# Reordering a cast, moving one stage by a slot, and halving the last tile in a linear attention and mixer kernel

## The chip, the core and the metric

One core of a Trainium2 chip. Times are device microseconds of one execution; lower is better. All runs told here are fast (granted TensorE clock 0.995 to 1.0). Below, PE is TensorE, PEld its weight loads, DVE is VectorE, ACT is ScalarE, POOL is GpSimd, SP is SyncE; a "q" after the name is that engine's instruction queue where it issues a DMA.

## The reference

Eight batches, eight heads, 576 rows, 64 columns per head. Linear attention, then a token mixer and a channel mixer:

```python
k_p, q_p = phi(k), phi(q)                    # phi(x) = elu(x) + 1
kv  = einsum('bhsd,bhse->bhde', k_p, v);  z = k_p.sum(axis=2)
x   = einsum('bhsd,bhde->bhse', q_p, kv) / (einsum('bhsd,bhd->bhs', q_p, z)[..., None] + 1e-6)
# heads side by side: x is [8, 576, 512]
h   = relu(x.T @ w_tok1) @ w_tok2;  u = x + h.T          # token mixer
out = u + relu(u @ w_ch1) @ w_ch2                        # channel mixer, 512 -> 1536 -> 512
```

## The kernel before

The program is a hand-made order: a list of large pieces of PE work ("big": blocks of the channel mixer), and between them, at numbered slots, the small pieces of the next batch ("fill"). Each slot of the channel mixer is four matmuls of 512 columns. Batches go in pairs, as the last 64 rows of two batches share one tile.

Names used below: k' and q' are `k_p` and `q_p`; kv is the product of k' and v; the numerators (nd) are the products of q' with kv and z; mm1 and mm2 are the two products of the token mixer; uT is u transposed, uTt the same for the tile of the tail rows that two batches share; cr and crt are relu(u @ w_ch1), again for whole tiles and for the tail. PSUM is the memory that PE writes its results to; to evict a block is to copy it from there, which frees its buffer. A "row" of a timeline is a run of like instructions merged into one line.

```python
def vcast(n, c, copy=nc.scalar.copy):            # L151: v to bf16, beside a column of ones
    copy(out=vs[:, js, :, 0:D], in_=raw["v", n % 2][:, js]...)

def kv(n, cs):                                   # L169: 72 quarter matmuls, c = 0 then c = 1
    for c in cs:
        for t in range(T):
            for a, i in QUARTERS:
                nc.tensor.matmul(out=ps[half[i], a, c], lhsT=kp[half[a], c, t, i],
                                 rhs=vs[half[a], 2 * c + i, t], ...)
    ...                                          # L175: two ACT copies into kvbd

def mm3(n, mc, kjs=range(NDM), dve=False):       # one block of the channel mixer, L475
    if kjs[0] == 0:
        part_of[mc] = ps_big.tile([128, 512], FP32, name="c_ps", tag="big")    # 4 buffers
    ...
    if kjs[-1] == NDM - 1 and dve:
        nc.vector.tensor_scalar(out=cr[b][:, mc, :], in0=ps, ..., op0=ALU.max)  # L479
    elif kjs[-1] == NDM - 1:
        nc.scalar.activation(out=cr[b][:, mc, :], in_=ps, func=AF.Relu)         # L482

# batch 1 prepared beside batch 0 (slots at0): qt0 11, qt1 13, vc 13, kv 14, ...
late = [("vc", lambda: vcast(1, 0)), ("vc", lambda: vcast(1, 1, nc.vector.tensor_copy))]
for nm, fn in first[1:3] + late + first[0:1] + first[3:]:     # first = kv, qt0, qt1, nd...
    fill += [(at0[nm], fn)]

# batch 2 prepared beside batch 1; DVE evicts blocks 4 and 7 (counted from 0)
big = ... + [lambda mc=mc: mm3(1, mc, dve=mc in (4, 7)) for mc in range(3, NCH)] + m3t + m4(0, [4, 5, 6, 7, 8])
at1 = {"kv": 7, "nd00": 9, ..., "mm1": 16, "mm2a": 17, "mm2b": 18, "mm2t": 20, "uta": 17, "utb": 18}
fill = [(s, lambda g=g: phi("k", 2, g)) for g, s in ((0, 0), (1, 2))]
fill += [(4, lambda: vcast(2, 0)), (5, lambda: vcast(2, 1, nc.vector.tensor_copy))]
# [...]
# last pair: tiles of the second channel product in the order 8, 4, 5, 6, 7; each one ends in
nc.vector.tensor_tensor(out=o, in0=ps, in1=u[b][:, r, :], op=ALU.add)           # L518
# and one store of 64 rows on SP and one on ACT                                  # L523
```

## Time and profile before

| | before |
|---|---|
| time, median of the runs of the first measurement | 267.39 us (266.95 to 267.62, 4 runs) |
| span in the profile | 265.8 us |
| PE busy | 256.6 us, 97% |
| PE waits on the cast of v | 0.8 us, two times |

How to read it: PE is full, so the span is PE's work plus its gaps plus the two ends (the start before PE's first useful matmul, and the add and the store after its last).

### The profile page before, as it was taken

Reading aid. Unit: us, or ns where it says so; the run is one execution under the profiler, and the core shown is the slowest. Engines: PE = TensorE matmul, PEld = TensorE weight load, DVE = VectorE, ACT = ScalarE, POOL = GpSimd, SP = SyncE. Lnnn points to the kernel's source line nnn. Section 1 sums busy time; section 2 is a strip of 40 time slices with the busy share of each in tenths; the row PEclk is TensorE's granted clock in tenths of the full one; section 3 lists DMA queues with packets and bytes.
Section 4 is the critical chain, followed back from the end, with each engine's and each line's share of the span. In section 5 each row is a group of like instructions: output and inputs, shape, how many; then the busy total and the mean of one; then the engine's idle time right before and its main releaser. Section 6 shows DMA issues by size and latency. Waiting matters only on the chain.

```text
span 265.8 us, 5142 instructions
## 1 busy us (share of the span) xinstructions
PE 256.6 (97%) x2107; PEld 134.1 (50%) x2107; DVE 158.2 (60%) x311; ACT 132.8 (50%) x200; POOL 33.4 (13%) x54
## 2 busy tenths in 40 slices
PE   7999989999999999999999999999999999999992
PEld 2684445554744454455554554455564554444641
DVE  5764967966839686948684286939684272320121
ACT  5645768268464358525771358435870363036300
POOL 9720300120002300030001300030001300000000
PEclk9999999999999999999999999999999999999999
DMA  7999999399406995899999990671074500730043
GB/s 260 246 203 280 373 214 399 133 191 402 168 2 125 191 383 201 108 239 369 285 411 210 258 409 32 143 171 36 2 135 116 118 2 0 162 94 2 0 118 79
DMA packets 49927, 48.34 MB, mean 182 GB/s; under 512 B 30256, under 2 KB 35248, under 8 KB 49904
## 3 DMA queue, kind: packets, MB, share of 16 engines
q1 hardware_dynamic: 41824, 35.53, 46.8%
q0 software_dynamic: 7440, 11.44, 20.4%
q10 hardware_dynamic: 640, 1.05, 1.2%
q8 instruction: 16, 0.26, 0.4%
q14 instruction: 7, 0.06, 0.1%
HBM read 35.85 MB, written 9.44 MB: 170 GB/s over the span
## 4 chain that ended last, share of the span: by engine, by line
PE 87%; DMA 4%; DVE 3%; ACT 2%; issue 1%; POOL 0%; ACTq 0%; POOLq 0%
PE h_ps L501 34%; PE c_ps L475 27%; PE a_ps L248 5%; PE h_ps L261 5%; DMA uTt<-ut 4%; PE c_ps L489 4%; PE bank L545 3%; PE nd_ps L210 3%; PE kv_ps L169 2%; ACT e L125 1%; PE bank L363 1%; PE bank L413 1%; DVE e L139 1%; DVE vs L151 1%; PE bank L385 1%
## 5 line engine op out<-in xcount | busy, mean ns | idle before, releaser
L482 ACT ACTIVATE cr<-c_ps 128x512 bf16<-128x512 f32 x91 | 53.5, 598 | 78.0 <-PE c_ps L475 77.8
L475 PE MATMUL c_ps<-uT,wc 128*128 128x512 bf16 x384 | 91.5, 379 | 0.4 <-ACT uT L444 0.4
L501 PE MATMUL h_ps<-wc,cr 128*128 128x512 bf16 x384 | 87.4, 379 | 0.0
L501 PEld LDWEIGHTS <-cr 128*128 128x128 bf16 x384 | 37.1, 98 | 43.0
L475 PEld LDWEIGHTS <-wc 128*128 128x128 bf16 x384 | 35.7, 98 | 36.5 <-issue 1.0
L518 DVE TENSOR_TENSOR o_sb<-h_ps,u 128x512 f32<-128x512 f32 x32 | 21.8, 688 | 28.0 <-PE h_ps L501 27.9
L523 POOL DMA_DIRECT2D out_dram<-o_sb x24 | 14.9, 627 | 154.1 <-DVE o_sb L518 154.1
L222 DVE TENSOR_TENSOR x<-nd_ps,den 128x512 bf16<-128x512 f32 (+1 forms) x42 | 25.3, 602 | 1.4
L139 DVE TENSOR_SCALAR e<-e 128x1152 bf16<-128x1152 bf16 x30 | 13.9, 463 | 12.7 <-ACT e L125 12.6
L125 ACT ACTIVATE e<-k_raw 128x1152 bf16<-128x1152 f32 x16 | 18.7, 1170 | 2.3 <-DMA k_raw<-in_k_dram 2.3
L125 ACT ACTIVATE e<-q_raw 128x1152 bf16<-128x1152 f32 x16 | 18.5, 1161 | 1.6 <-DMA q_raw<-in_q_dram 1.4
L273 DVE TENSOR_TENSOR u<-h_ps,x 128x1024 bf16<-128x1024 f32 x12 | 14.4, 1219 | 7.2 <-PE h_ps L261 7.1
L219 DVE TENSOR_SCALAR den<-nd_ps 128x8 f32<-128x8 f32 (+1 forms) x42 | 6.8, 163 | 19.2 <-PE nd_ps L210 18.6
L261 PE MATMUL h_ps<-ar,w2p 128*128 128x512 bf16 x60 | 16.0, 379 | 0.1
L210 PEld LDWEIGHTS <-qT 128*128 128x128 bf16 x140 | 11.4, 98 | 9.3 <-issue 0.2
L210 PE MATMUL nd_ps<-kvbd,qT 128*128 128x130 bf16 x140 | 15.1, 223 | 0.0
L248 PE MATMUL a_ps<-x,w 128*128 128x512 bf16 x56 | 14.4, 379 | 0.0
L151 ACT CAST vs<-v_raw 128x1152 bf16<-128x1152 f32 x12 | 13.9, 1160 | 0.0
L528 DVE TENSOR_TENSOR o_sb<-h_ps,ut 128x512 f32<-128x512 f32 x4 | 2.8, 690 | 18.7 <-PE h_ps L501 18.7
L251 ACT ACTIVATE ar<-a_ps 128x512 bf16<-128x512 f32 x14 | 7.6, 595 | 12.1 <-PE a_ps L248 12.1
L140 DVE TENSOR_TENSOR qp<-e,y 128x1152 bf16<-128x1152 bf16 x16 | 12.1, 758 | 0.6
L131 DVE TENSOR_SCALAR y<-q_raw 128x1152 bf16<-128x1152 f32 x16 | 12.1, 756 | 0.3
(102 smaller groups left out, 218.1 us busy)
## 6 DMA issues: line engine op xcount, KB each, us to landing
k_raw<-in_k_dram SPq DMA_DIRECT2D x16, 576.0 KB, 9.0
q_raw<-in_q_dram SPq DMA_DIRECT2D x16, 576.0 KB, 7.0
v_raw<-in_v_dram SPq DMA_DIRECT2D x14, 576.0 KB, 11.0
out_dram<-o_sb POOLq DMA_DIRECT2D x24, 256.0 KB, 4.7
wc<-in_moe_w_ch_dram POOLq DMA_DIRECT2D x8, 384.0 KB, 9.8
out_dram<-o_sb SPq DMA_DIRECT2D x10, 128.0 KB, 2.3
out_dram<-o_sb ACTq DMA_DIRECT2D x8, 128.0 KB, 2.6
out_dram<-o_sb POOLq DMA_DIRECT2D x6, 128.0 KB, 7.0
```

What stands on the lines that cost most here:

```text
L125: nc.scalar.activation(out=e, in_=f, func=AF.Exp)
L139: nc.vector.tensor_scalar(out=e, in0=e, scalar1=1.0, scalar2=None, op0=ALU.min)
L151: copy(out=vs[:, js, :, 0:D], in_=raw["v", n % 2][:, js].rearrange("p j (t d) -> p j t d", t=T))
L210: nc.tensor.matmul(out=o[:, a], lhsT=qT[b][:, t0:t0 + 128], rhs=kvbd[b][:, c, a], start=True, stop=True)
L222: nc.vector.tensor_tensor(out=x[b][:, rs[0]:rs[0] + m, HG * D * g:HG * D * (g + 1)].rearrange("p r (h d) -> p r h d", h=HG), in0=v_[:, :, ...
L248: nc.tensor.matmul(out=ps[:, mt], lhsT=w1t[:, b, ms] if r == R else w1[:, r, ms], rhs=x[b][:, r, :], start=(r == 0), stop=(r == R))
L261: nc.tensor.matmul(out=ps[:, i], lhsT=w2v(kt, r, b), rhs=ar[b][:, kt, :], start=(kt == 0), stop=(kt == NT - 1 and not add))
L475: nc.tensor.matmul(out=ps, lhsT=wc1[:, kj, 128 * mc:128 * mc + 128], rhs=uT[b][:, :, kj], start=(kj == 0), stop=(kj == NDM - 1))
L482: nc.scalar.activation(out=cr[b][:, mc, :], in_=ps, func=AF.Relu)
L501: nc.tensor.matmul(out=ps, lhsT=crt[:, kc, :] if t == 8 else cr[b][:, kc, 128 * r:128 * r + 128], rhs=wc2[:, kc, :], start=(kc == 0), stop ...
L518: nc.vector.tensor_tensor(out=o, in0=ps, in1=u[b][:, r, :], op=ALU.add)
L523: (nc.scalar if last and e else put).dma_start(out=outv[2 * p + b, :, 2 * r0 + e:2 * r0 + e + 2 * m - 1:2], in_=live["o"][half[e], 0:m])
```

## The change

Three parts: the cast of v in batch 1 goes ahead of the copies of q' (so that DVE casts while PE transposes); kv of batch 2 goes one slot later with everything that hangs on it; and the very last tile is computed, added and stored in two halves of 256 columns.

```diff
+    def mm4_last(c):
+        p, b, r, cs = B // 2 - 1, 1, R - 1, COLS[c]
+        ps = ps_big.tile([128, 512], FP32, name="h2_ps", tag="big")[:, 0:DM // 2]
+        for kc in range(NCH):
+            nc.tensor.matmul(out=ps, lhsT=cr[b][:, kc, 128 * r:128 * r + 128],
+                             rhs=wc2[:, kc, cs], start=(kc == 0), stop=(kc == NCH - 1))
+        o = outp.tile([128, 2, DM], FP32, name="o_sb", tag="o_sb")[:, 0, 0:DM // 2]
+        nc.vector.tensor_tensor(out=o, in0=ps, in1=u[b][:, r, cs], op=ALU.add)
+        for e in range(2):
+            (nc.scalar if e else nc.sync).dma_start(out=outv[2 * p + b, :, 2 * r + e, cs],
+                                                    in_=o[half[e]])
-    for nm, fn in first[1:3] + late + first[0:1] + first[3:]:
+    for nm, fn in first[1:2] + late + first[2:3] + first[0:1] + first[3:]:
-    at1 = {"kv": 7, "nd00": 9, "nd01": 10, "nd10": 11, "nd11": 12, "nd20": 13, "nd21": 14,
-           "mm1": 16, "mm2a": 17, "mm2b": 18, "mm2t": 20, "uta": 17, "utb": 18}
+    at1 = {"kv": 8, "nd00": 10, "nd01": 11, "nd10": 12, "nd11": 13, "nd20": 14, "nd21": 15,
+           "mm1": 17, "mm2a": 18, "mm2b": 19, "mm2t": 21, "uta": 18, "utb": 19}
-    fill += [(s, lambda g=g: phi("q", 3, g)) for g, s in ((0, 19), (1, 21))]
-    fill += [(22, lambda: qtr_dma(3)), (22, lambda: load_all(4, "qkv"))]
-    fill += [(s, lambda g=g: prep_k(3, g)) for g, s in ((0, 24), (1, 26))]
+    fill += [(s, lambda g=g: phi("q", 3, g)) for g, s in ((0, 19), (1, 22))]
+    fill += [(23, lambda: qtr_dma(3)), (23, lambda: load_all(4, "qkv"))]
+    fill += [(s, lambda g=g: prep_k(3, g)) for g, s in ((0, 24), (1, 27))]
-            big = m3(n) + m3t + m4(p, [4, 5, 6, 7, 8] if n + 1 < B else [8, 4, 5, 6, 7])
+            big = m3(n) + m3t + m4(p, [4, 5, 6, 7, 8])
+            if n + 1 == B:
+                big = m3(n) + m3t + m4(p, [8, 4, 5, 6]) + [lambda: mm4_last(0), lambda: mm4_last(1)]
```

The lines of the changed kernel after this function are numbered 13 higher; the two new lines that count are 537 (matmul) and 540 (add), with the stores at 542.

## The prediction

> **What bounds the kernel now.** I read the page first (busy shares, chain of waits), then the waits of TensorE after the start-up, then the timeline around each place that the change touches. The change is a matter of tenths of a microsecond, so shares do not decide it; single instructions do.
>
> The page, span and busy shares:
>
> ```profile
> span 265.8 us, 5142 instructions
> PE 256.6 (97%) x2107; PEld 134.1 (50%) x2107; DVE 158.2 (60%) x311; ACT 132.8 (50%) x200; POOL 33.4 (13%) x54
> ```
>
> TensorE (PE) is busy 97% of the span, and the chain of waits is PE for 87% of it. So PE's work is the floor, and only two things can be gained: gaps between PE's instructions, and what comes before its first and after its last matmul. The waits of PE alone, from 20 us to the end (who waited for whom: us in total, times, longest), the three largest:
>
> ```profile
> PE kv_ps L169 <- DVE vs L151: 0.8, 2, 0.5
> PE tp L180 <- DVE qp L140: 0.6, 2, 0.4
> PE c_ps L475 <- ACT uT L444: 0.4, 1, 0.4
> ```
>
> The largest is the product k'v (line 169) waiting for VectorE's cast of v (line 151), two times: in batch 1 and in batch 2. The first two parts of the change aim at these. Timeline of batch 1 (start us, duration us, engine, line, output<-input, count, idle before):
>
> ```profile
> 36.21 0.76 DVE L140 TENSOR_TENSOR qp<-e,y 128x1152 bf16<-128x1152 bf16 x1
> 37.54 1.03 PE L501 MATMUL h_ps<-wc,cr 128*128 128x512 bf16 x4
> 37.74 0.82 DVE L187 COPY qT<-tp 128x640 bf16<-128x640 bf16 x2 [0.77 <-PE tp L180]
> 38.48 0.75 DVE L151 CAST vs<-v_raw 128x1152 bf16<-128x1152 f32 x1
> 38.50 0.48 PE L169 MATMUL kv_ps<-vs,kp 64*64 64x65 bf16 x36
> 39.29 0.48 PE L169 MATMUL kv_ps<-vs,kp 64*64 64x65 bf16 x36 [0.30 <-DVE vs L151]
> 39.70 1.04 PE L501 MATMUL h_ps<-wc,cr 128*128 128x512 bf16 x4
> ```
>
> VectorE (DVE) idles 0.77 us for PE's transposes, copies them out, and only then casts v; the second 36 matmuls start right as the cast ends. Batch 2:
>
> ```profile
> 62.32 0.68 DVE L479 TENSOR_SCALAR cr<-c_ps 128x512 bf16<-128x512 f32 x1
> 62.70 0.48 PE L169 MATMUL kv_ps<-vs,kp 64*64 64x65 bf16 x36
> 62.92 0.75 DVE L151 CAST vs<-v_raw 128x1152 bf16<-128x1152 f32 x1
> 63.73 0.48 PE L169 MATMUL kv_ps<-vs,kp 64*64 64x65 bf16 x36 [0.54 <-DVE vs L151]
> 64.14 1.41 PEld L475 LDWEIGHTS <-wc 128*128 128x128 bf16 x8
> 64.14 1.90 PE L475 MATMUL c_ps<-uT,wc 128*128 128x512 bf16 x8
> ```
>
> Here DVE is busy all the way: the eviction of the fifth channel block (line 479) and then the cast. A kv without a wait, batch 3:
>
> ```profile
> 79.26 1.23 DVE L273 TENSOR_TENSOR u<-h_ps,x 128x1024 bf16<-128x1024 f32 x1 [0.50 <-PE h_ps L261]
> 88.99 1.89 PE L475 MATMUL c_ps<-uT,wc 128*128 128x512 bf16 x8
> 89.56 0.76 DVE L140 TENSOR_TENSOR kp<-e,y 128x1152 bf16<-128x1152 bf16 x1
> 90.81 0.78 PE L169 MATMUL kv_ps<-vs,kp 64*64 64x65 bf16 x72
> 91.52 1.90 PE L475 MATMUL c_ps<-uT,wc 128*128 128x512 bf16 x8
> ```
>
> All 72 run together, and from kv's start to the next matmul it is 91.52 - 90.81 = 0.71 us. But k' of batch 3 is ready (89.56 + 0.76 = 90.32) only 0.49 us before kv begins. Finally the end:
>
> ```profile
> 261.15 0.69 DVE L518 TENSOR_TENSOR o_sb<-h_ps,u 128x512 f32<-128x512 f32 x1 [1.90 <-PE h_ps L501]
> out_dram<-o_sb SPq DMA_DIRECT2D x3, 128.0 KB, 2.3
> out_dram<-o_sb ACTq DMA_DIRECT2D x3, 128.0 KB, 2.6
> ```
>
> After PE's last matmul one add of 0.69 us and a store that lands after 2.3 and 2.6 us lie bare.
>
> **What the Trainium skill says.** "TensorE: Matmul & The Clock Gate", section "Step-by-step: what each phase is for": matmuls stay in program order, only weight loads are pulled ahead. So a kv that waits holds everything behind it, as above. The same page, "Back-to-back issue gap", gives N/2.4 + 2.5 ns: 216 ns for 512 columns, 109 ns for 256. The trace agrees: eight 512-column matmuls take 1.73 us in the chain (0.216 each), twenty 256-column ones at line 413 take 2.18 us (0.109 each). "VectorE: DVE Perf Modes", the section on the TRN2 errata, gives (N + 151)/0.96 ns for an fp32 tensor_tensor add: 691 ns for 512, 424 ns for 256. The trace has 688 and 690 ns at lines 518 and 528, and 424 ns for the 128x256 form of line 222, also a read of PSUM. "DMA: Bandwidth & Descriptors", "Latency and other measured facts", puts a fixed cost of about 2 us on a DMA, most of it the receipt from HBM; so halving a store saves only the moving part. Here that part is visible: in half-microsecond windows after 262.0 the DMA share is 0, 0.08, 0.90, 0.96, 0.07, so about 1.0 us of moving.
>
> **The change part by part.** The order of instructions on each engine, built for both kernels, shows little more than the diff: on DVE the cast of batch 1 moves ahead of its two qT copies and nothing else moves except the last add; ScalarE (ACT) has one eviction more before kv's copies in batch 2; PE has the batch 2 chain one slot of four 512-column matmuls later.
>
> *A, batch 1.* q' ends at 36.97. The cast can start then: v was issued at 19.7 and 20.3 us and landed at most 14.6 us later, by about 34.9. It runs to about 37.7, while DVE was idle for the transposes anyway, so the qT copies still start at about 37.74. kv's first half keeps 38.50 (PE's four matmuls of 37.54 stream until 38.41). The second half follows at once: next matmul at 38.50 + 0.71 = 39.21 in place of 39.70. Gain 0.49 us. What follows (kvbd copies on ACT, numerators, q' of batch 2) hangs on PE and moves with it; q of batch 2 lands at an absolute time (ACT starts its exponential at 43.23 after a wait for the DMA), but DVE needs that result only at 47.74, with more than 2 us of slack.
>
> *B, batch 2.* The last four matmuls ahead of kv start at 61.66 and stream to 61.66 + 4 x 0.216 = 62.52. A kv without waits would end at 62.52 + 0.09 + 0.71 = 63.32, where the next matmul now starts at 64.14: the two waits cost 0.82 us. But with kv a slot later, the ninth channel block comes first, and it takes the PSUM buffer of the fifth (four buffers in rotation; the built order shows that it waits on DVE). DVE frees that at 62.32 + 0.68 = 63.00. So PE starts at about 63.06 and not 62.52, streams to 63.92, and runs kv with v cast (63.67) by then: to 63.92 + 0.09 + 0.71 = 64.72. Before, the same point (kv and ninth block done) was 64.14 + 0.86 = 65.00. Gain 0.28 us in place of 0.82.
>
> *C, what B hands on to batch 3.* Numerators, first mixer product and its u now come after one more slot: 0.86 later in program order, less the 0.28: 0.58 us later in time. From the u at 79.26 to k' at 90.32 DVE has no gap in the timeline: seventeen instructions, whose durations sum to 11.9 us in a stretch of 11.06 (each starts a little before the modelled end of the one before). So k' ends at 90.90 relative to A's shift, with the semaphore (0.06 us from the cast's end to kv in batch 2) 90.96. PE gets to kv of batch 3 at 90.81 - 0.28 = 90.53, and its second half 0.29 us later, 90.82. It waits about 0.14 us. B and C together: 0.28 - 0.14 = 0.14 us. Later batches resynchronise (DVE idles 2.77 us for PE before the numerators of batch 3).
>
> *D, the end.* 24 matmuls of 256 columns take 24 x 0.109 = 2.62 us in place of 12 x 0.216 = 2.59: lost 0.02. The last add: 0.69 to 0.42, gained 0.27. The last store: half the bytes in as many pieces (64 rows on each of two queues, 1 KB in place of 2 KB). If the moving time halves, 0.5 us; if it goes by pieces, nothing; I take 0.3, an estimate. The first half's store is issued about 1.3 us earlier and out of the way. Sum 0.55 us.
>
> Total: 0.49 + 0.14 + 0.55 = 1.18 us. 267.51 - 1.18 = 266.3 us.
>
> **The rivals.** (1) No new wait: B gains the full 0.82 and C nothing. Then 267.51 - 0.49 - 0.82 - 0.55 = 265.65. For it speaks that steady batches show kv without any wait; against it, DVE's eviction at 62.32, which nothing in the change moves. (2) DVE becomes the bound: the shift of B falls on the gapless stretch from 79 to 90 us and costs as much at kv of batch 3 as B gained. Then 266.5. It is the closest rival; 0.14 us here is the difference of numbers near 90 with errors of about 0.1 each. (3) The store is all fixed latency, and its end does not move: D gains 0.25 and the time is 266.6. (4) A is hidden by a landing of q or by DVE's own load between 41 and 51 us: 266.8. Against it: DVE's numerator rhythm there is PE's (1.10 us for four matmuls and four short ones), and no transfer is waited for by PE.
>
> **Range and chances.** All rivals lie between 265.65 and 266.8; runs of the kernel before spread over 0.34 us. I put 8 in 10 on 265.7 to 266.9. Two per cent is 5.35 us, more than four times the largest sum, and nothing on the path can cost as much: faster 0.01, same 0.98, slower 0.01.
>
> **What would show it.** A right: kv of batch 1 as 72 matmuls in one row, no wait for the cast. B right: the wait of kv for the cast gone, and in its place about half a microsecond of PE before the ninth channel block, put down to DVE line 479. C right: a short stop inside kv of batch 3, put down to k'. D right: a last add of 0.42 us, and the last store landing in about 2.0 to 2.4 us. I am wrong if DVE starts the chain of batch 2 at another time relative to PE (B and C change together), or if a transposing DMA that now starts 0.58 us later holds up the numerators of batch 3.

## More of the kernel before

One more stretch of the chain of waits (start us, us, what) was there to be read, and comes back later:

```profile
119.69 11.95 DMA uTt<-ut
131.68 1.05 PE c_ps L489 x16
```

It is the transposing DMA for the tail rows of batches 2 and 3. PE was busy nearly all the time that it was in flight, so it looked harmless.

## The result, and the profile after

| | before | after |
|---|---|---|
| median, first measurement | 267.39 us (4 runs) | 266.34 us (265.98 to 266.39, 4 runs) |
| ratio of fast runs, 95% interval | | 0.9960 (0.9942 to 0.9977) |
| measured once more, in the last set of runs | 267.63 us (11 runs) | 266.09 us (265.83 to 266.47, 6 runs) |
| ratio, 95% interval | | 0.9944 (0.9931 to 0.9958) |
| span in the first profile | 265.8 us | 264.5 us |

A ratio is the mean time of one kernel's fast runs over that of the other's of the same rounds, so not quite the ratio of the medians. The time for before, 267.51, was the median of three runs; the fourth made it 267.39.

The waits of PE in the changed kernel from 20 us on (who waited for whom: us in total, times, longest), the second and third of six:

```profile
PE c_ps L475 <- ACT uT L444: 0.4, 1, 0.4
PE c_ps L475 <- DVE cr L479: 0.4, 1, 0.4
```

Both waits for the cast (line 151) are gone. The second of these lines is new: it is the wait on the eviction at line 479. (The list counts 0.38 us from the modelled end of the matmul before; the ninth block could have followed that matmul 0.216 us after its start, at 62.36, so PE lost 0.54 us.) The timeline of batch 1 in the changed kernel (start us, duration us, engine, line, output<-input, count, idle before):

```profile
37.21 0.76 DVE L151 CAST vs<-v_raw 128x1152 bf16<-128x1152 f32 x1
...
38.82 0.78 PE L169 MATMUL kv_ps<-vs,kp 64*64 64x65 bf16 x72
39.53 1.04 PE L501 MATMUL h_ps<-wc,cr 128*128 128x512 bf16 x4
```

The cast now runs at 37.21, while PE transposes (37.35 to 38.03); the copies follow at 38.06. So all 72 matmuls of kv stand in one row: 39.53 - 38.82 = 0.71 us to the next matmul, where it was 1.20. Batch 2:

```profile
62.16 0.68 DVE L479 TENSOR_SCALAR cr<-c_ps 128x512 bf16<-128x512 f32 x1
...
62.90 1.02 PE L475 MATMUL c_ps<-uT,wc 128*128 128x512 bf16 x4 [0.38 <-DVE cr L479]
...
63.85 0.78 PE L169 MATMUL kv_ps<-vs,kp 64*64 64x65 bf16 x72
```

PE waits for the eviction to end (62.84) and starts at 62.90; the cast (62.76 to 63.51) is then in time for kv at 63.85. The next block starts at 64.56. Batch 3:

```profile
89.98 0.76 DVE L140 TENSOR_TENSOR kp<-e,y 128x1152 bf16<-128x1152 bf16 x1
90.36 0.91 PE L169 MATMUL kv_ps<-vs,kp 64*64 64x65 bf16 x72
```

kv of batch 3 takes 0.91 where a kv without a stop takes 0.78. No wait is listed for it, and the 72 stay merged into one row, as the stop is too short for both views; only the duration, and k' ending at 90.74 after kv's start, show it. The end of the kernel, first the timeline and then the issues of stores (KB each, median us from issue to landing):

```profile
260.69 0.42 DVE L540 TENSOR_TENSOR o_sb<-h_ps,u 128x256 f32<-128x256 f32 x1 [0.89 <-PE h_ps L537]
```

```profile
out_dram<-o_sb SPq DMA_DIRECT2D x2, 64.0 KB, 2.0
out_dram<-o_sb ACTq DMA_DIRECT2D x2, 64.0 KB, 2.3
```

The add fell from 0.69 to 0.42. The landing times just above are medians over both halves' stores. For the last half alone they are 1.9 (SP) and 2.2 us (ACT), where the last whole tile of the kernel before took 2.3 and 2.6: 0.4 less.

**Where the time is, stretch by stretch.** Whole times differ by 1 us and more between runs of one kernel (before alone: 266.98 to 267.96 in one set; eviction first: 264.69 to 266.25), so tenths can't be read from them. Stretches of PE's timeline can. I cut every profile at the same matmuls: the first matmul of kv in batch 1; the first of the token mixer of batch 1 (line 248); the first of kv of batch 4; of kv of batch 5; the first of the tail tile of the last pair (line 501, from crt); the end of the last add; the end of the span.

| run | start to kv 1 | kv 1 to mixer 1 | to kv 4 | kv 4 to kv 5 | to the last tiles | to the last add's end | to the end |
|---|---|---|---|---|---|---|---|
| before | 38.50 | 8.49 | 69.98 | 32.59 | 98.44 | 13.84 | 3.96 |
| after | 38.82 | 8.01 | 69.83 | 32.40 | 98.45 | 13.60 | 3.39 |
| after, again | 38.52 | 8.00 | 69.85 | 32.30 | 98.45 | 13.61 | 3.38 |
| cast alone | 39.11 | 8.01 | 69.98 | 32.30 | 98.45 | 13.85 | 3.91 |
| slot alone | 37.95 | 8.49 | 69.84 | 32.55 | 98.44 | 13.85 | 3.99 |
| tail alone | 39.18 | 8.49 | 69.99 | 32.64 | 98.45 | 13.60 | 3.36 |
| mixer back | 39.24 | 8.01 | 69.70 | 32.45 | 98.45 | 13.61 | 3.45 |
| eviction first | 39.07 | 8.01 | 69.15 | 32.78 | 98.44 | 13.61 | 3.44 |
| DVE more, in after | 38.99 | 8.01 | 70.64 | 32.30 | 98.44 | 13.60 | 3.42 |
| DVE more, in before | 38.34 | 8.49 | 70.05 | 32.65 | 98.44 | 13.84 | 3.89 |
| all, cut at 384 | 38.61 | 8.01 | 69.01 | 32.30 | 98.45 | 13.47 | 3.55 |
| loads later | 39.11 | 8.01 | 69.83 | 32.31 | 98.45 | 13.60 | 3.40 |
| best | 38.70 | 8.00 | 69.02 | 32.30 | 98.45 | 13.60 | 3.44 |

(The spans are given to a tenth, so the last column is good to 0.1.) In seven of these traces (after again, cast, slot, tail, mixer back, loads later, best) the first of the twelve matmuls of the tail tile has no record: the trace shows eleven, after a gap of 0.27 us where the others show 0.06. There the cut is set 0.216 us before the first one recorded. Four columns repeat to 0.02 us wherever the kernels agree in them. Two vary from trace to trace for other reasons: the start, where the differences arise ahead of the instructions that the edits touch, and the stretch between kv of batch 4 and of batch 5, of which more below.

### The profile page after: what moved, and what is told of

It is laid out like the page before. It is cut to its first block, busy times and chain, and to the rows that moved or that the text cites. A ratio compares the mean times of both kernels' runs of the same rounds, so it can differ in the third digit from the quotient of the medians.

```text
span 264.5 us, 5173 instructions
## 1 busy us (share of the span) xinstructions
PE 255.8 (97%) x2119; PEld 135.0 (51%) x2119; DVE 158.3 (60%) x312; ACT 132.8 (50%) x200; POOL 33.0 (12%) x54
## 4 chain that ended last, share of the span: by engine, by line
PE 87%; DVE 5%; DMA 3%; ACT 2%; POOL 1%; issue 1%; ACTq 0%; POOLq 0%
PE h_ps L501 34%; PE c_ps L475 27%; PE a_ps L248 6%; PE h_ps L261 5%; PE c_ps L489 4%; PE nd_ps L210 3%; DMA cr<-in_v_dram 3%; PE kv_ps L169 2%; DVE y L131 1%; PE h_ps L537 1%; DVE cr L479 1%; DVE kp L140 1%; PE bank L363 1%; PE bank L413 1%; DVE e L139 1%
## 5 line engine op out<-in xcount | busy, mean ns | idle before, releaser
L501 PE MATMUL h_ps<-wc,cr 128*128 128x512 bf16 x372 | 84.9, 379 | 0.0
L501 PEld LDWEIGHTS <-cr 128*128 128x128 bf16 x372 | 36.0, 98 | 41.3
L518 DVE TENSOR_TENSOR o_sb<-h_ps,u 128x512 f32<-128x512 f32 x31 | 21.1, 688 | 23.1 <-PE h_ps L501 23.0
L139 DVE TENSOR_SCALAR e<-e 128x1152 bf16<-128x1152 bf16 x30 | 13.9, 462 | 12.5 <-ACT e L125 12.4
```

The source lines that it names most:

```text
L139: nc.vector.tensor_scalar(out=e, in0=e, scalar1=1.0, scalar2=None, op0=ALU.min)
L501: nc.tensor.matmul(out=ps, lhsT=crt[:, kc, :] if t == 8 else cr[b][:, kc, 128 * r:128 * r + 128], rhs=wc2[:, kc, :], start=(kc == 0), stop ...
```

## The experiments

**Each part alone.** Three kernels: before with the changed order of the cast only; before with the changed at1, phi, transposing and k' slots only; before with mm4_last only. Their edits are the corresponding hunks of the diff above. First the cast:

```diff
-    for nm, fn in first[1:3] + late + first[0:1] + first[3:]:
+    for nm, fn in first[1:2] + late + first[2:3] + first[0:1] + first[3:]:
```

> Part A alone (cast of v ahead of q's copies in batch 1). Theory: kv of batch 1 runs as one row of 72, the next matmul starts 0.71 us after kv's first in place of 1.20, so 0.49 us less than the kernel before (267.4 to 266.9), with nothing else moved. Rival (the copies of q' or the landing of q give it back before the numerators): under 0.15 us less.

Measured: kv of batch 1 is one row of 72, and the stretch to the mixer is 8.01 in place of 8.49 us: 0.48 us gained, all of it kept up to kv of batch 4 (69.98, as before). The time, 267.23 against 267.42 us, ratio 0.9995 (0.9982 to 1.0008), doesn't resolve it: the interval goes from a gain of 0.48, just what the trace shows, to a loss of 0.21 us. In its profile the start took 0.6 us more than in before's, ahead of anything that the cast can touch.

Then the slot (the hunks of at1, phi q, qtr_dma, load_all and prep_k):

```diff
-    at1 = {"kv": 7, "nd00": 9, [...] "mm1": 16, "mm2a": 17, "mm2b": 18, [...]}
+    at1 = {"kv": 8, "nd00": 10, [...] "mm1": 17, "mm2a": 18, "mm2b": 19, [...]}
```

> Part B alone (kv of batch 2 one slot later with its whole chain). Theory: the cast's wait (0.54) goes, a wait of about 0.4 for the eviction on VectorE line 479 comes, and kv of batch 3 stops 0.1 to 0.2 us for k': net 0.14 us less than before (0.0 to 0.3). Rival (no new waits): 0.82 us less. Rival (the chain into batch 3 takes all): 0 or more time.

Measured: 69.84 in place of 69.98, so 0.14 us, with both new waits in the timeline: 0.38 us for line 479 before the ninth block, and a kv of batch 3 of 0.91 us. The time shows no gain: 267.59 against 267.42, ratio 1.0011 (0.9996 to 1.0025). That speaks against 0.82 us, and is a hair outside of 0.14 (the interval ends at a gain of 0.11). I hold to the trace for the stretch and leave open whether chance at the start made these six runs slow.

Then the tail (mm4_last and the last list of big):

```diff
+            if n + 1 == B:
+                big = m3(n) + m3t + m4(p, [8, 4, 5, 6]) + [lambda: mm4_last(0), lambda: mm4_last(1)]
```

> The halved last tile alone. Theory: the last add is 0.42 in place of 0.69 us, the last store lands 0.3 us sooner after its issue, PE loses 0.03: 0.54 us less than before. Rival (the store is fixed latency): 0.25 us less.

Measured: from the last tiles to the end of the last add 13.60 in place of 13.84, and from there to the end 3.36 in place of 3.96 us. The time is 266.87 against 267.42, ratio 0.9979 (0.9963 to 0.9995), 0.56 us gained with 0.13 to 0.99 in the interval. This is the only part whose gain the times show by themselves.

The times of the three parts together give 0.13 - 0.29 + 0.56 = 0.40 us, where their stretches give 1.4 and the whole change measured 1.07 and 1.5. Chance at the start is large enough for that difference, but with one trace of each kernel it is not shown to be the reason. What follows on single parts rests on the stretches.

**Where the second store's gain comes from.** The DMA engines' share of time at the end (columns after the window: its length, then busy us of PE, PEld, DVE, ACT, POOL with counts, granted clock, DMA share, GB/s), before:

```profile
263.00:263.60 0.60, 0.00 (x0) 0.00 (x0) 0.00 (x0) 0.00 (x0) 0.00 (x0) 1.00 0.95 188
263.60:264.20 0.60, 0.00 (x0) 0.00 (x0) 0.00 (x0) 0.00 (x0) 0.00 (x0) 1.00 0.66 236
```

and after:

```profile
261.80:262.40 0.60, 0.00 (x0) 0.00 (x0) 0.00 (x0) 0.00 (x0) 0.00 (x0) 1.00 0.20 44
262.40:263.00 0.60, 0.00 (x0) 0.00 (x0) 0.00 (x0) 0.00 (x0) 0.00 (x0) 1.00 0.78 174
```

Share times length, over these windows and one before them in before's trace with a share of 0.06: 1.0 us of moving before, 0.6 after. Both traces have 128 pieces for the last store, of 2048 bytes (123 ns each on average) and of 1024 bytes (72 ns). So the moving falls with the bytes, though not quite to half, and not with the number of pieces. From the first piece to the last it takes 262.98 to 264.16 us before and 262.26 to 263.00 after, 0.44 less, and the ACT store lands 0.42 sooner after its issue (2.64 to 2.22). The rest of this stretch's gain, some 0.1 us, comes after the landing: from there to the end of the span it is 1.27 to 1.30 us in the four traces with a whole last tile and 1.15 to 1.18 in all with a cut one. No run here shows why.

**Is the stop in kv of batch 3 that chain?** First the mixer of batch 2 put back to its old slots, kv and numerators left one slot later:

```diff
-           "mm1": 17, "mm2a": 18, "mm2b": 19, "mm2t": 21, "uta": 18, "utb": 19}
+           "mm1": 16, "mm2a": 17, "mm2b": 18, "mm2t": 20, "uta": 17, "utb": 18}
-    fill += [(s, lambda g=g: phi("q", 3, g)) for g, s in ((0, 19), (1, 22))]   # [...] 23, 27
+    fill += [(s, lambda g=g: phi("q", 3, g)) for g, s in ((0, 19), (1, 21))]   # [...] 22, 26
```

(Cut: qtr_dma and load_all go back from slot 23 to 22 and the second prep_k from 27 to 26.)

> The changed kernel with the token mixer's products of batch 2, its transposes and the preparation of batch 3 put back to the slots that they had before; kv and the numerators stay one slot later. Theory: u of batch 2 is 0.86 us earlier against PE's other work, so k' of batch 3 is ready before kv and its stop goes: 0.14 us less than the changed kernel, 1.2 to 1.3 less than before. The wait for line 479 stays. Rival (the stop in kv of batch 3 has nothing to do with that chain, or mm1 now waits for the last numerators): no gain, or a new wait of PE at line 248.

Measured: 69.70 in place of 69.83 us, and kv of batch 3 lasts 0.78 again (start 90.78, with k' ending at 90.30):

```profile
90.78 0.78 PE L169 MATMUL kv_ps<-vs,kp 64*64 64x65 bf16 x72
```

The wait for line 479 stays at 0.4. 0.13 us gained, no new wait at line 248. The time is 0.9958 (0.9942 to 0.9973) of before.

Then the suspected cost doubled: one DVE instruction of the gapless stretch is repeated (it writes a y that nobody reads, so the result stays right), in the changed kernel and in the one before.

```diff
-    fill += [(s, lambda g=g: prep_k(3, g)) for g, s in ((0, 24), (1, 27))]
+    fill += [(24, lambda: prep_k(3, 0)), (24, lambda: phi_add("k", 3, 0, 2)), (27, lambda: prep_k(3, 1))]
```

> The changed kernel with one VectorE instruction of 0.75 us repeated (idempotent, its result unused) inside the gapless stretch ahead of k' of batch 3. Theory: the stop in kv of batch 3 grows by the start-to-start time of such an instruction, 0.67 us, to about 0.8 us, and the kernel with it. Rival (the stretch isn't what kv waits for): no change.

Measured: kv of batch 3 falls in two.

```profile
90.54 0.48 PE L169 MATMUL kv_ps<-vs,kp 64*64 64x65 bf16 x36
90.95 0.76 DVE L140 TENSOR_TENSOR kp<-e,y 128x1152 bf16<-128x1152 bf16 x1
91.76 0.48 PE L169 MATMUL kv_ps<-vs,kp 64*64 64x65 bf16 x36 [0.74 <-DVE kp L140]
```

The second half starts 1.22 us after the first, where 0.29 is enough: a stop of 0.93 us. The stretch is 70.64 in place of 69.83, so 0.81 us more, somewhat over the 0.67 expected: from the repeat's start to the next one's it is 0.67, but the instruction ahead of it, at 87.60, also holds DVE longer, 0.80 us to the repeat at 88.40, where it was 0.68 without. The time loses half or more of what the change had gained (0.998 of before, 0.9967 to 0.9993).

> The kernel before with the same repeated instruction at the same place. Theory: there kv's second half had 0.29 + 0.43 = 0.72 us of slack, so 0.67 us more on VectorE costs 0.0 to 0.1 us. Rival: it costs what it costs in the changed kernel.

Measured: in the kernel before, the same instruction costs 70.05 - 69.98 = 0.07 us; kv of batch 3 lasts 0.85 in place of 0.78. Time 0.9995 (0.9983 to 1.0007) of before. The repeat puts DVE back by 0.79 us here (the instruction ahead of it holds DVE for 0.79 us, 86.86 to 87.65, in place of 0.68, and the repeat itself for 0.68), and the slack was 0.72: the 0.49 us between k' and kv that the prediction read, plus 0.29 to kv's second half, less 0.06 for the semaphore. The difference is the 0.07. So the slack was there, and the changed kernel had used it up.

**Is the wait at line 479 a matter of order?** The changed kernel, but the second half of k' is made after the fifth block's eviction, not before it:

```diff
-    fill = [(s, lambda g=g: phi("k", 2, g)) for g, s in ((0, 0), (1, 2))]
+    fill = [(0, lambda: phi("k", 2, 0)), (2, lambda: phi_exp("k", 2, 2, 2)),
+            (4, lambda: phi_add("k", 2, 2, 2)), (4, lambda: phi_end("k", 2, 2, 2))]
```

> The changed kernel, but VectorE evicts the fifth channel block of batch 2 (line 479) before it makes the second half of k', not after. Theory: the PSUM buffer comes free about 1.3 us sooner, so the ninth block needn't wait (0.4 to 0.5 us of PE gained), and the cast ends when it did, just in time for kv's second half: 0.4 to 0.55 us less than the changed kernel. Rival (the wait only moves to the cast or to k'): under 0.1 us gained, with a wait inside kv of batch 2.

Measured: 69.15 in place of 69.83 us, 0.68 gained, more than expected. The timeline of batch 2:

```profile
56.85 6.64 PE L475 MATMUL c_ps<-uT,wc 128*128 128x512 bf16 x30
...
60.39 0.68 DVE L479 TENSOR_SCALAR cr<-c_ps 128x512 bf16<-128x512 f32 x1
...
62.82 0.76 DVE L151 CAST vs<-v_raw 128x1152 bf16<-128x1152 f32 x1
...
63.42 0.78 PE L169 MATMUL kv_ps<-vs,kp 64*64 64x65 bf16 x72
```

The eviction comes 60.39 - 56.85 = 3.54 us after the start of that row of matmuls, where it was 62.16 - 56.60 = 5.56 in the changed kernel; the thirty matmuls ahead of kv run without a break (29 x 0.216 + 0.38 = 6.64), and kv's second half starts about when the cast ends. The 0.68 is 0.54 for the wait at line 479 and 0.14 for a shorter one that the prediction had not counted: the eighth block too had waited for its buffer (26 matmuls took 5.92 us in before and after, where 25 x 0.216 + 0.38 is 5.78). In the built order of this kernel the eighth block takes the buffer that DVE frees early and the ninth the one that ACT frees. The trace fits that: the eighth block's first matmul is due at 56.85 + 22 x 0.216 = 61.60 and isn't late, while ACT ends its eviction of the fourth block only at 61.70. The time is 265.37 against 267.83 us, 0.9911 (0.9895 to 0.9927).

**All of it, with the last tile cut at column 384.** The two edits above together, and in mm4_last:

```diff
-        p, b, r, cs = B // 2 - 1, 1, R - 1, COLS[c]
+        p, b, r, cs = B // 2 - 1, 1, R - 1, (slice(0, 384), slice(384, DM))[c]
```

> The changed kernel with the mixer of batch 2 back at its old slots, the fifth block's eviction ahead of the second half of k', and the last tile cut at column 384, not 256. Theory: 0.14 + 0.45 us as in the single runs, and at the end the last add falls from 0.42 to about 0.29 us and the last store by 0.1 us: about 0.8 us less than the changed kernel, some 265.5. Rival (the pieces collide): less than 0.4 us gained.

Measured: 69.01 us to kv of batch 4, which is 0.82 less than after, as 0.68 + 0.13 says. The smaller last add gains 0.13 (13.47), but the end after it grows from about 3.4 to 3.55: the last store is issued right behind the first piece's (on ACT 0.22 us after the add's end, elsewhere 0.03), and lands 2.18 us after its issue where it was 2.22, although its bytes are half of those. Time 265.44 against 267.83, 0.9912 (0.9898 to 0.9925). Cutting the tile more unevenly isn't worth it.

**What makes the stretch from kv 4 to kv 5 vary?** In eleven profiles it was 32.30 to 32.78 us. The tile of the tail rows' transposed u (uTt), before:

```profile
L464 SPq DMA_TRANSPOSE uTt<-ut x1: 4254/4254/4254, 119.7 to 119.7; - x1
DMA to landing us min/median/max: 11.9/11.9/11.9
```

119.7 + 11.9 = 131.6, and the matmuls that need it start at 131.68, 0.29 us later than PE could: the list of waits put that down to nobody. In "eviction first", the longest case, it is listed:

```profile
131.13 1.05 PE L489 MATMUL c_ps<-uTt,wc 128*128 128x128 bf16 x16 [0.32 <-DMA uTt<-ut]
```

The transfer stands on SP behind six loads for batch 5. So the loads were put after it, in the changed kernel:

```diff
-                fill += [(12 + d, lambda: load_all(5, "qkv"))]
+                fill += [(16, lambda: load_all(5, "qkv"))]
```

> The changed kernel with the loads of q, k and v of batch 5 issued after the transposing DMA of the batch 2 and 3 tails (uTt), not before it. Seen in the traces so far: from kv of batch 4 to kv of batch 5 it is 32.30 us in some runs and up to 32.78 in others, with a wait for uTt, whose transfer lands 11 to 12 us after its issue. Theory: that spread is a wait for this transfer queued behind the loads; with the order turned it lands in under 6 us, the stretch is 32.30 us, and the mean time falls by 0.1 to 0.3 us. Rival (the spread is of another kind): the stretch keeps its spread.

Measured, the same tile:

```profile
L464 SPq DMA_TRANSPOSE uTt<-ut x1: 3169/3169/3169, 114.2 to 114.2; - x1
DMA to landing us min/median/max: 5.2/5.2/5.2
```

It lands after 5.2 us, 12 us ahead of its use, and the stretch is 32.31. The other traces agree one by one: in the seven whose stretch is longer than 32.30 the matmuls of line 489 start 0.04 or 0.05 us after the landing, and in the four with 32.30 the transfer had landed 0.18 to 0.31 us before they started. The cause of this spread is shown. The mean time did not fall, though: 266.29 us against 266.09 of the changed kernel on the same chip. Its profile has the start 0.6 us later; with a wait of 0.0 to 0.5 us the effect is under what the times resolve.

> The changed kernel itself once more, as the yardstick on the same chip. Theory: stretches as in its first trace (batch 1's kv to the mixer 8.01 us, to kv of batch 4 69.83), and a time 1.0 to 1.5 us below the kernel before. Rival (its gain in the first measurement was the chance of a good start-up): under 0.7.

Measured: 8.00 and 69.85 us, and a time of 0.9944 (0.9931 to 0.9958) of before: about 1.5 us less. The first measurement said 1.07 us. Both are in the expected range, or at its edge.

**The best version.** The changed kernel with the mixer of batch 2 back, the eviction first and the loads later; the last tile in equal halves.

> The changed kernel with the three remedies together (mixer of batch 2 at its old slots, fifth block evicted ahead of the second half of k', loads of batch 5 after uTt), the last tile in equal halves. Theory: from the first mixer product of batch 1 to kv of batch 4 69.0 us as against 69.83, the next stretch 32.30, the end as in the changed kernel: 0.8 to 1.1 us less than the changed kernel, about 265.3. Rival: the gains don't add, less than 0.5.

Measured: 69.02 and 32.30 us, 265.38 us median (265.01 to 267.30, 6 runs) against 267.63 of before, ratio 0.9926 (0.9903 to 0.9950) with one run of 267.3 among the six; the other five are 265.01 to 265.67. The changed kernel stood at 266.09 on the same chip. It beats the kernel before. Against the changed kernel the medians differ by 0.71 us and the ratios by 0.5, less than the 0.8 to 1.1 expected; five of its six runs lie below all six of the changed kernel, but with the sixth the two intervals overlap. So the traces show the gain (69.02 against 69.85 us), and the times alone don't settle it. Nor do they show that the mixer back and the later loads add to the eviction first, which by itself measured 0.9911 of before on another chip.

## Why the prediction was right or wrong, point by point

The time, 266.34 us, against 266.3 predicted, and inside of the range; the repetition at 266.09 too. That the first is within 0.1 us is partly luck: the stretches say that the sum was 0.2 us too small, and runs of one kernel differ by more than that.

- A, the cast in batch 1: 0.49 predicted, 0.48 measured in the stretch, alone and with the rest. Right in mechanism and size. Rival 4 (hidden by a landing or DVE's load) falls: the stretches after it are unchanged.
- B and C: 0.14 predicted, 0.13 to 0.15 measured. The new wait at line 479 began and ended where the prediction had it (0.06 us after the eviction's end), which rules rival 1 out; the cure by order, which gave 0.68 us, shows the cause. The stop inside kv of batch 3 was predicted as 0.14 us and is 0.13 (0.91 against 0.78); putting the mixer back removes it, and more work on DVE lengthens it, so the gapless stretch is its cause. Rival 2 was near but fell: the carry-over takes half of what B gains, not all. The delay handed on is as predicted too: u starts at 79.68 in place of 79.26, and all that goes before batch 2 was 0.16 us earlier in this trace (start 0.32 later, A 0.48 sooner), so 0.42 + 0.16 = 0.58 us. But 0.14 was a difference of two such numbers, each with an error of about 0.1 by the prediction's own word; to hit it within 0.01 was luck as well.
- The prediction expected that stop to be "put down to k'" in the profile. It wasn't: the row of 72 hides it until it is long enough, as in the run with more DVE work.
- D, the tail: the step that was mis-sized is the store, "if the moving time halves, 0.5 us; if it goes by pieces, nothing; I take 0.3". After the last add's end the kernels with a whole last tile need 3.94 us on average (3.96, 3.91, 3.99, 3.89), and those with halves 3.41 (after, after again, tail alone, mixer back, eviction first, more DVE in after, loads later, best: 3.36 to 3.45). So it is 0.53 us. The moving fell by some 0.4 (landing 2.64 to 2.22), and 0.1 came after the landing, a term that the prediction didn't have and whose cause stays open. Rival 3, a store of fixed latency, falls. The add and PE's part came as predicted: 13.84 to 13.60 is 0.24, against 0.27 - 0.02. D is 0.77 in the traces, not 0.55.
- So the sum by the traces is 0.48 + 0.15 + 0.77 = 1.40 us, not 1.18. The times say 1.07 and 1.5 us in two measurements. Two places that the prediction didn't name vary by enough to lie between: the start (37.95 to 39.24 us to kv of batch 1) and the wait for uTt (0 to 0.48 us). The second was visible in the chain of waits of before and was passed over as PE being busy.
- Left open: what makes the start vary by over 1 us. Nearly all of the variation is there before the first token mixer of batch 0 (15.7 to 17.0 us), while weights and inputs are still loading; no experiment here takes it apart.

## What to carry to other kernels

Moving a stage to escape one wait moves all that hangs on it: look for which buffer the work now in front needs, and whether an engine that looked idle on average has a gapless stretch between the moved stage and its next use. In an order of instructions that is made by hand, the cheaper cure is often to swap two instructions on the engine that is late (the eviction ahead of k': 0.68 us) rather than to move the one that waits (0.14 us). And tenths of a microsecond are read from stretches of the trace that repeat to 0.02 us, not from times that scatter by 1 us and more.

## What the Trainium skill lacked or had wrong

- "TensorE: Matmul & The Clock Gate", section "Back-to-back issue gap": it gives a sustained roofline of about 131 ns per matmul of 512 columns and about 81 ns per one of 128 in a stream of weight loads and matmuls, and calls N/2.4 + 2.5 the isolated gap. In these runs streams of exactly such pairs go at 216 ns (eight in 1.73 us) and 56 ns (48 in 2.68 us at line 489): the formula holds, the sustained figures don't.
- "DMA: Bandwidth & Descriptors", section "DMA Transpose (X-bar)": no word on how long a small transpose takes behind loads on the same queue. Here the same 128x512 bf16 transpose landed after 10.7 to 12.5 us behind six loads of 576 KB, and after 5.2 and 5.3 us ahead of them.
